# First expert of a top-1 mixture: 320 slots in the other experts' form, 128 slots stationary, a branch for 64 more

## The chip, the core and the metric

One core of one Trainium2 chip runs the whole kernel. The metric is the device time of one execution in microseconds. Engines are named as the profile names them: PE (TensorE), DVE (VectorE), ACT (ScalarE), POOL (GpSimd), SP (SyncE).

## What is computed

```python
# attention: 4 batches x 8 heads x 768 tokens x 64, float32
mask = (q_bucket == k_bucket)            # 6-bit hashes of q @ proj and k @ proj
attn = softmax(where(mask, q @ k.T / 8, -1e9));  x = attn @ v   # x: 3072 tokens x 512
# mixture, 8 experts, one expert per token
logits = x @ w_gate;  e_idx = argmax(logits)
gate_w = softmax(logits)[e_idx];  eom = sigmoid(x @ w_output_gate)
for e in range(8):
    m = e_idx == e
    h = relu(x[m] @ w1[e])               # 512 -> 1024
    out[m] = gate_w[m] * eom[m, e] * (h @ w2[e])   # 1024 -> 512
```

How many tokens an expert gets depends on the data, so the kernel sorts tokens into slots of each expert and has a general path behind it for whatever doesn't fit.

## The kernel before

Every product of the mixture is made of three matmuls (`product`, L389): both operands are split into a high and a low part, and high x high, high x low and low x high are summed. A block of 128 output columns of layer 1 over 512 inputs is thus 4 x 3 = 12 matmuls, a block of layer 2 over 1024 inputs is 8 x 3 = 24.

The experts are worked through in the order of their size. Experts 1 to 7 have one form. In layer 1 (`up`) the weights are stationary and the tokens' slots stream, as many columns as the expert's width; four steps of two blocks each write one PSUM tile `ps_s` (two buffers). ACT takes the high part (`hh`, L412), DVE the low part (`hl`, L415). In layer 2 (`down`) w2 is stationary, the slots stream again, DVE turns the result (`yt`, L452), it goes to DRAM and comes back in rows (`yo`), is scaled on ACT and scattered to the output by POOL (`send_rows`) during the next expert.

While expert r runs, its hooks prepare expert r+1 (`turned`, `next_w1`) and fetch rows for r+2. A chunk of 128 tokens is fetched by four indirect gathers `xq` (L329), issued by POOL. DVE transposes the chunk (`xt`, L342), POOL makes its high part (`xh`, L345), DVE the low part (`xlo`, L346). `pace` (L327) makes each next gather wait for the block finished last. DVE clears the PSUM tile of the next block in order behind all this work (`clear`), so the first block of expert r+1 can start only when DVE has come past expert r+1's last `xt`, `xlo` and the first half of its own `yt`. The order of each engine is the order in which the code is written; nothing reorders it.

The first expert (r = 0) is chosen while the attention still runs, as the largest after three of the four batches. It has 512 slots. The first 256 go through layer 1 during the end of the attention (`fill`, L1212: 96 matmuls of 256 columns), then through layer 2 with the slots stationary (`down_rows`: 48 matmuls of 512 columns). The other 256 are gathered, turned (`turn`, L305), go through layer 1 with the weights stationary (again 96 of 256) and layer 2 with slots stationary (`all_rows`, again 48 of 512). In this second half the hooks issue the first gathers for expert 2, after `slot_rows` has made the row numbers `idx`.

Of the kernel before, what the change touches and what calls it, by code (L numbers as in the profile page):

```python
# [33 lines left out]
WIDTHS = ((512,), (480, 448, 428), (448, 420, 404), (416, 400, 384), (384, 376, 364), (384, 364, 348),  # L34
# [6 lines left out]
CAP0 = CH * EARLY  # L41

# [25 lines left out]
def lsh_attention_then_moe(  # L68
# [73 lines left out]
    def triangle():  # L142

        trif = gp.tile([P, P], F32, name="t_tri")
# [30 lines left out]
    def load_weights(shape, src):  # L175
# [3 lines left out]
        else:  # L179

            raw = f32(gp.tile([P, NCC, CAP0], F32R, name=("xh0", "xlo0")[raws[-1] - 2])).rearrange("p a b -> p (a b)")
# [94 lines left out]
    pace = []  # L276

# [12 lines left out]
    def gather(idx, n=CH, ntok=NTOK, pool=gp, bufs=NCH):  # L290

        xg = pool.tile([CH, DM], F32, name="xg", bufs=bufs)
        nc.gpsimd.indirect_dma_start(out=xg[0:n], out_offset=None, in_=x_dram[0:ntok, :],
                                     in_offset=bass.IndirectOffsetOnAxis(ap=idx[0:n], axis=0))
        return xg, n

    def new_x0():
        return [gp.tile([P, NCC, CAP0], F32R, name=n) for n in ("xh0", "xlo0")]

    def turn(xgn, xs, c0, early=False):  # L300

        xg, n = xgn
        px = (ps_m if early else ps_t).tile([P, NCC, CH], F32, name="ps_m" if early else "ps_t")
        for cc in range(NCC):
            nc.tensor.transpose(px[:, cc, 0:n], xg[0:n].rearrange("n (p b) -> n b p", b=NCC)[:, cc], ident[0:n, 0:n])  # L305
        xh, xlo = (x[:, :, c0:c0 + n] for x in xs)
        nc.scalar.copy(xh, px[:, :, 0:n])
        nc.vector.tensor_tensor(xlo, px[:, :, 0:n], f32(xh), ALU.subtract)
# [86 lines left out]
    def up(w1s, xs, hs, fs, n, midway=None, r=None):  # L395
# [18 lines left out]
        def lows():  # L414
            nc.vector.scalar_tensor_tensor(hl, ph, 0.0, f32(hh), ALU.max, ALU.subtract)  # L415
            if r:
                clear()
            elif r == 0 and fs[-1] == NFB - 1:
                clear()
                clear()  # L420
# [9 lines left out]
    def send(r, a, n, py, sid):  # L430

        yo = mp.tile([CH, DM], F32, name="yo", bufs=4)
        nc.scalar.activation(yo[0:n].rearrange("n (a g f) -> n g a f", a=NB32, g=NCC),
                             py[0:n].rearrange("n (g a f) -> n g a f", a=NB32, g=NCC), AF.Copy,
                             scale=tacc[0:n, 1, r, a:a + 1])
        scatter(
            out=out[:, :], out_offset=bass.IndirectOffsetOnAxis(ap=sid[0:n, r, a:a + 1], axis=0),
# [18 lines left out]
    def to_dram(r, yt):  # L456

        nb = CAPS[r] // 32
        for k in range(NB32):
            nc.sync.dma_start(y_dram[0:CAPS[r], k * P:(k + 1) * P].rearrange("(t i) x -> i t x", i=32),  # L460
                              yt[32 * k:32 * k + 32, 0:nb].rearrange("i t g f -> i t (g f)"))

    def to_rows(r):

        for a, n in enumerate(chunks(r)):
# [49 lines left out]
    with ExitStack() as actx:  # L515
# [487 lines left out]
        def pick():  # L1003
# [10 lines left out]
            nc.vector.scalar_tensor_tensor(base, lead, float(CAP0), base, ALU.mult, ALU.max)  # L1014

        def lead_slots(a):

            tm = gp.tile([P, EARLY, E], F32, name="o_ls")
            nc.vector.tensor_tensor(tm, tacc_e[:, 0, :, a:a + EARLY].rearrange("p e a -> p a e"),
                                    lead[:, None, :].broadcast_to([P, EARLY, E]), ALU.mult)  # L1020
            gd = gp.tile([P, EARLY], F32, name="o_gd")
            nc.vector.tensor_reduce(gd, tm, AX.X, ALU.add)
            gid = gp.tile([P, EARLY], U32, name="gid0")
            nc.vector.tensor_scalar(gid, gd, -1.0, 0.0, ALU.add, ALU.max)
# [15 lines left out]
        def load_experts():  # L1040
# [4 lines left out]
            for i in range(1, E):  # L1045
                load_expert(idi, i)
# [45 lines left out]
        def early_gather():  # L1092
            gid = lead_slots(0)
            early["xg"] = [gather(gid[:, a:a + 1], CH, NTOK - S) for a in range(EARLY)]
# [29 lines left out]
        for a in range(EARLY):  # L1124
            plan(late + 20 + 2 * a, lambda a=a: early_turn(a))
# [86 lines left out]
        def fill(f, midway=None):  # L1212
            lows.append(up(early["w1"], early["x"], hs, [f], CAP0, midway))
# [47 lines left out]
        fill(7)  # L1261
        r["hot"]()
        r["right"]()
        rows(NP - 1, 1, False)
        low()
        r["softmax_sum"]()
        r["chosen"]()
        r["gates"]()

    mp = ctx.enter_context(tc.tile_pool(name="mp", bufs=1, reuse_waits="tile"))  # L1270
    with order_ctx:
        x0 = new_x0()
        pys = [ps_s.tile([P, 2, 512], F32, name="ps_s")[:, 0] for c in range(EARLY)]
        def first_table():
            last["table"](0, 1)
            last["entries"](0, 1)
            gid0 = lead_slots(EARLY)
            rows = [gather(gid0[:, a:a + 1]) for a in range(EARLY)]
            pick = picks()
            last["heavy"]()  # L1280
            order()
            return rows, pick

        for c in range(EARLY):
            for f in range(0, NFB, 2):
                if c == 0 and f == 2:
                    down_rows(c, CH, w2s, hs, pys[c], [f])
                    xg, pick = first_table()
                    down_rows(c, CH, w2s, hs, pys[c], [f + 1])
                else:  # L1290
                    down_rows(c, CH, w2s, hs, pys[c], [f, f + 1])
                if c == 0 and f == 6:
                    last["table"](1, 3)
                    ordered_table(0)
                    gid = sources(mp, tacc)
# [215 lines left out]
```

## Time and profile before

| | |
|---|---|
| time, median of 3 runs | 728.63 us (728.61 to 728.78) |
| the profiled execution's own time | 727.21 us |
| its span in the trace | 725.4 us |
| mean granted clock of PE | 0.997 |
| PE busy | 715.5 us (99% of the span) |
| DVE, ACT, POOL busy | 514.0, 460.0, 385.7 us |

The span is the time from the first to the last instruction of the profiled execution; 1.8 us of its own time lie around it. A share of busy time is an average over the whole span: an engine at 53% can still be the one that is waited for in a stretch of 30 us. In a timeline the busy time of a matmul overlaps the next one's; what a matmul costs is the distance between two starts.

### The profile page before, as it was taken

The page shows a single profiled execution, that of the slowest core. Times are in us where ns is not written, and L with a number is a line of the kernel's source. Part 1 is how long each engine was busy: PE and PEld are TensorE (multiplying, and loading weights), DVE is VectorE, ACT ScalarE, POOL GpSimd, SP SyncE. Part 2 cuts the span into 40 slices and gives each one's busy share as a digit, 9 for nine tenths or more (in the row PEclk, how much of TensorE's full clock was granted, in tenths as well). Part 3 has the DMA queues.
Part 4 walks back from the last instruction along what each step waited for, and adds up shares of the span by engine and source line. Part 5 has one row for each costly group of instructions (what it writes and reads, how often), then busy time and mean ns, then how long its engine had stood idle before and what let it go on. Part 6 is the DMA issues. An engine that isn't in the chain of part 4 may idle for free.

```text
span 725.4 us, 14193 instructions
## 1 busy us (share of the span) xinstructions
PE 715.5 (99%) x4671; PEld 595.9 (82%) x4671; DVE 514.0 (71%) x1148; ACT 460.0 (63%) x983; POOL 385.7 (53%) x446
## 2 busy tenths in 40 slices
PE   8999999999999999999999999999999999999996
PEld 6777767778687687776776787989999999999995
DVE  7877768878977877977899757546665647567740
ACT  8788887888877888887888762235061617153341
POOL 7655554454753554644568551455657474846212
PEclk9999999999999999999999999999999999999998
DMA  4565655555663654665465232564585867668641
GB/s 153 147 148 123 148 124 118 137 113 119 137 155 80 144 147 88 144 146 98 123 163 135 88 82 51 174 216 149 159 259 183 247 191 234 212 217 275 213 155 41
DMA packets 98020, 109.45 MB, mean 151 GB/s; under 512 B 58729, under 2 KB 70153, under 8 KB 97920
## 3 DMA queue, kind: packets, MB, share of 16 engines
q1 hardware_dynamic: 92576, 94.81, 49.4%
q0 software_dynamic: 5200, 13.31, 5.5%
q8 instruction: 60, 0.98, 0.6%
q14 instruction: 40, 0.33, 0.1%
q10 hardware_dynamic: 144, 0.02, 0.0%
HBM read 64.60 MB, written 18.32 MB: 114 GB/s over the span
## 4 chain that ended last, share of the span: by engine, by line
PE 83%; issue 6%; DVE 4%; DMA 3%; POOL 2%; SPq 1%; ACT 1%; POOLq 0%; DVEq 0%; ACTq 0%
PE ps_s L393 28%; PE ps_s L710 17%; PE ps_a L784 17%; PE ps_t L762 16%; PE ps_m L566 2%; DVE sc L714 1%; POOL out_dram L426 1%; PE ps_m L818 1%; DMA yo<-y_dram 1%; PE ps_m L393 1%; PE ps_a L393 1%; DMA yr<-xl 1%; POOL yr L612 1%; PE ps_t L305 0%; DMA xg<-x_dram,gid 0%
## 5 line engine op out<-in xcount | busy, mean ns | idle before, releaser
L746 POOL TENSOR_SCALAR sc<-sc,rsum 128x768 f32<-128x768 f32 x192 | 184.5, 975 | 182.2 <-DVE rsum L744 133.5
L714 DVE TENSOR_SCALAR_CACHE_REDUCE sc<-ps_s 128x768 f32<-128x768 f32 x192 | 181.1, 948 | 37.8 <-PE ps_s L710 32.3
L766 ACT COPY pts<-ps_t 128x384 f32<-128x384 f32 x375 | 161.3, 482 | 73.2 <-PE ps_t L762 72.6
L725 ACT ACTIVATE sc<-sc,mn 128x768 f32<-128x768 f32 (+1 forms) x223 | 187.6, 847 | 0.7 <-DVE sc L714 0.7
L762 PE MATMUL ps_t<-ident,sc 128*128 128x128 f32 x1134 | 156.7, 274 | 0.8 <-ACT pts L766 0.4
L762 PEld LDWEIGHTS ps_t<-ident,sc 128*128 128x128 f32 x1134 | 132.6, 140 | 26.4 <-POOL sc L746 10.4
L784 PE MATMUL ps_a<-pts,vt 128*64 128x384 f32 x768 | 130.9, 490 | 0.0
L412 ACT ACTIVATE hh<-ps_s 128x768 fp32r<-128x768 f32 (+6 forms) x40 | 29.3, 733 | 138.7 <-PE ps_s L393 138.7
L329 POOL DMA_INDIRECT xq<-x_dram,idx x75 | 89.5, 1193 | 52.0 <-ACT hh L412 20.0
L710 PE MATMUL ps_s<-xr,xl 128*128 128x384 f32 x384 | 114.2, 378 | 1.1 <-DVE sc L714 0.8
L784 PEld LDWEIGHTS ps_a<-pts,vt 128*64 128x64 f32 x768 | 52.3, 137 | 64.9 <-issue 56.4
L710 PE MATMUL ps_s<-yr,yl 76*128 76x384 f32 x384 | 99.3, 340 | 0.4 <-POOL yr L612 0.3
L393 PE MATMUL ps_s<-xh,w1h 128*128 128x256 f32 (+7 forms) x288 | 93.6, 325 | 0.0
L393 PE MATMUL ps_s<-xlo,w1h 128*128 128x256 f32 (+7 forms) x288 | 93.2, 324 | 0.0
L393 PE MATMUL ps_s<-xh,w1l 128*128 128x256 f32 (+7 forms) x288 | 93.1, 323 | 0.0
L415 DVE SCALAR_TENSOR_TENSOR hl<-ps_s,hh 128x768 fp32r<-128x768 f32 (+6 forms) x40 | 34.4, 859 | 62.3 <-ACT hh L412 62.3
L710 PEld LDWEIGHTS ps_s<-yr,yl 76*128 76x128 f32 x384 | 69.7, 189 | 1.0 <-POOL yr L612 0.5
L426 POOL DMA_INDIRECT out_dram<-yo,sid x27 | 28.4, 1050 | 70.2 <-ACT yo L472 55.7
L393 PE MATMUL ps_s<-hl,w2h 128*128 128x428 f32 (+5 forms) x192 | 64.8, 338 | 0.0
L393 PE MATMUL ps_s<-hh,w2h 128*128 128x428 f32 (+5 forms) x192 | 64.7, 337 | 0.0
L393 PE MATMUL ps_s<-hh,w2l 128*128 128x428 f32 (+5 forms) x192 | 64.7, 337 | 0.0
L710 PEld LDWEIGHTS ps_s<-xr,xl 128*128 128x128 f32 x384 | 58.0, 191 | 7.4 <-issue 4.9
(229 smaller groups left out, 1022.5 us busy)
## 6 DMA issues: line engine op xcount, KB each, us to landing
w_raw<-in_w_dram SPq DMA_DIRECT2D x36, 512.0 KB
qk<-in_qkT_dram SPq DMA_DIRECT2D x32, 384.0 KB
xh<-in_w_dram SPq DMA_DIRECT2D x14, 512.0 KB
xlo<-in_w_dram SPq DMA_DIRECT2D x14, 512.0 KB
vt<-in_v_dram SPq DMA_DIRECT2D x16, 384.0 KB
xr<-xl SPq DMA_DIRECT2D x30, 192.0 KB
yr<-xl SPq DMA_DIRECT2D x30, 192.0 KB
xr<-yl SPq DMA_DIRECT2D x30, 192.0 KB
```

The source lines that it names most:

```text
L329: got = nc.gpsimd.indirect_dma_start(out=xq[:, k * P:(k + 1) * P], out_offset=None, in_=x_dram.rearrange("n (a f) -> (n a) f", a=NB32), in ...
L393: nc.tensor.matmul(ps, l, r, start=first and k == 0, stop=last and k == len(pairs) - 1)
L412: pace[:] = [nc.scalar.activation(hh, ph, AF.Relu).ins]
L415: nc.vector.scalar_tensor_tensor(hl, ph, 0.0, f32(hh), ALU.max, ALU.subtract)
L426: sent = nc.gpsimd.indirect_dma_start(**k).ins
L710: nc.tensor.matmul(ss[:, n, 0:HS], l[0:k, qs], r[0:k, n * HS:(n + 1) * HS], start=first, stop=not first)
L714: nc.vector.tensor_scalar(sc, ss[:, :, 0:HS], MASKED, None, ALU.min, ALU.min, accum_out=mn)
L725: nc.scalar.activation(pr, pr, AF.Exp, bias=mn, scale=-1.0, accum_out=total)
L746: nc.gpsimd.tensor_scalar(live[s0 + k], live[s0 + k], rs[:, k:k + 1], 0.0, ALU.mult, ALU.add)
L762: nc.tensor.transpose(tr[:, c], pr[:, (3 * h + c) * P:(3 * h + c + 1) * P], ident)
L766: (nc.vector.tensor_copy if shared and h else nc.scalar.copy)(pts[:, 3 * h:3 * h + 3, t * P:(t + 1) * P], tr)
L784: nc.tensor.matmul(st["av"][j * D:(j + 1) * D], st["v"][:, j, c], blocks[hb][j][:, c], start=(c == 0), stop=(c == NT - 1))
```

## The change

The first expert's slots go from 2 x 256 to 320 "near" slots and 128 "far" slots, with a branch for 64 more. The near slots take the early place: layer 1 in `fill`, now 320 columns wide, and layer 2 in the form of the other experts (`near_down`, four output blocks of 24 matmuls; `near_back` turns them on DVE; the rows are sent during expert 1). The far slots are stationary in both layers: `far_up` (24 matmuls of 512 columns into `ps_a` and `ps_m`), `far_relu`, eight transposes of h, `far_down` (24 of 512). Three `overflow` arms hold the work of slots 448 to 511 and are skipped when these are empty. One row in two scatters is a mix of a near and a far chunk (`mixed_ids`). The row numbers `idx` are made, and the first two gathers for expert 2 issued, inside `far_down`; the other gathers of expert 2 come at expert 1's own steps. Much of the table work that follows the attention is written in another order between the matmuls.

```diff
-WIDTHS = ((512,), (480, 448, 428), (448, 420, 404), (416, 400, 384), (384, 376, 364), (384, 364, 348),
+WIDTHS = ((512, 448), (480, 448, 428), (448, 420, 404), (416, 400, 384), (384, 376, 364), (384, 364, 348),
...
+NEAR = 320
+FAR = slice(NEAR, NEAR + CH)
+UPPER = slice(CH // 2, CH)
...
-            lows.append(up(early["w1"], early["x"], hs, [f], CAP0, midway))
+            lows.append(up(early["w1"], early["x"], hs, [f], NEAR, midway))
...
         copies()
+        rows(NP - 1, 1, False)
         fill(4, lambda: r["add_pair"](1, lp))
         r["best"]()
-        low()
         r["exps"]()
         r["choose"]()
-        fill(5)
-        fill(6, r["prefix"])
         low()
+        fill(5, r["prefix"])
         r["ranks"]()
         low()
+        fill(6)
         r["cols"]()
+        r["hot"]()
+        low()
         fill(7)
-        r["hot"]()
         r["right"]()
-        rows(NP - 1, 1, False)
-        low()
-        r["softmax_sum"]()
-        r["chosen"]()
-        r["gates"]()
...
-        pys = [ps_s.tile([P, 2, 512], F32, name="ps_s")[:, 0] for c in range(EARLY)]
-        def first_table():
...
-        for c in range(EARLY):
...
+        def near_down(py, d, f0, f1):
+            ds = slice(d * P, (d + 1) * P)
+            product(py[:, d % 2, 0:NEAR], [(w[0][:, ds], w[1][:, ds]) for w in w2s[f0:f1]],
+                    [(hs[0][:, f, 0:NEAR], hs[1][:, f, 0:NEAR]) for f in range(f0, f1)], f0 == 0, f1 == NFB)
+
+        def near_back(py, dp):
+            for j in range(2):
+                nc.vector.transpose(back[:, 0:NEAR // 32, 2 * dp + j],
+                                    py[:, j, 0:NEAR].rearrange("p (t i) -> p t i", i=32))
+
+        def far_up(pu, c0):
+            for i in range(2):
+                fs = slice(i * DM, (i + 1) * DM)
+                product(pu[i], [tuple(x[:, cc, c0:c0 + CH] for x in x0) for cc in range(NCC)],
+                        [(wh[:, fs], wl[:, fs]) for wh, wl in early["w1"]])
...
+        def far_relu(ps, pu):
+            rows = [mp.tile([CH, DM], F32, name="yo", bufs=4) for i in range(2)]
+            for i in range(2):
+                pace[:] = [nc.scalar.activation(rows[i][ps], pu[i][ps], AF.Relu).ins]
+            return [rows[f // NCC][ps, f % NCC * P:(f % NCC + 1) * P] for f in range(NFB)]
...
+        def overflow():
+            return tc.If(fits[0] < 1)
...
+        near_down(py, 0, 0, 1)
+        last["table"](0, 1)
+        order()
+        last["entries"](0, 1)
+        gid0 = lead_slots(len(near) - 1, 2)
+        rest = gather(gid0[:, 0:1])
+        more = gather(gid0[:, 1:2], CH, NTOK, CH // 2)
+        pick = picks()
+        idi = experts()
+        load_expert(idi, 1)
+        raw = [w1_load(1, cc) for cc in range(2)]
+        low()
+        last["softmax_sum"]()
+        last["chosen"]()
+        last["gates"]()
+        last["heavy"]()
+        near_down(py, 0, 1, NFB)
+        near_down(py, 1, 0, 6)
+        last["table"](1, 3)
+        near_down(py, 1, 6, NFB)
+        ordered_table(0)
+        gid = sources(mp, tacc)
+        ch = chunks(1)
+        first = [gather(gid[:, 1, a:a + 1], ch[a]) for a in range(2)]
+        near_back(py, 0)
+        py = ps_s.tile([P, 2, 512], F32, name="ps_s")
+        turn(rest, x0, 0)
+        near_down(py, 2, 0, 4)
+        turn(more, x0, CH)
+        near_down(py, 2, 4, NFB)
...
+        pu = [p.tile([CH, DM], F32, name=n) for p, n in ((ps_a, "ps_a"), (ps_m, "ps_m"))]
+        far_up(pu, 0)
+        h_rest = far_relu(slice(0, CH), pu)
+        read_fit(0)
+        with overflow():
+            far_up(spill, CH // 2)
+        xn = new_x()
+        turn(first[0], xn, 0)
+        turn(first[1], xn, CH)
+        near_down(py, 3, 0, 4)
+        w1n = [w1_split(wpool, raw[0])]
...
+        for i in range(2):
+            pt = ps_t.tile([P, NCC, CH], F32, name="ps_t")
+            for k in range(NCC):
+                nc.tensor.transpose(pt[:, k], h_rest[NCC * i + k], ident)
+            pace[:] = [halves([h[:, NCC * i:NCC * (i + 1), FAR] for h in hs], pt)]
...
+        near_down(py, 3, 4, NFB)
+        near_back(py, 1)
+        clear()
+        with overflow():
+            for f in range(NFB):
+                nc.tensor.transpose(pt[:, f], h_more[f], ident[UPPER, UPPER])
+        for a in range(2, len(ch)):
+            turn(first[a], xn, a * CH)
...
+        def far_down(py, cols, fs):
+            product(py, [(hs[0][:, f, cols], hs[1][:, f, cols]) for f in fs], [w2s[f] for f in fs],
+                    fs[0] == 0, fs[-1] == NFB - 1)
...
+        far_down(py, FAR, range(0, 4))
+        idx = slot_rows(ids, pick)
+        for a in range(len(chunks(2))):
+            fetch(a, 2)
+        gather_some(2)
+        read_fit(1)
+        far_down(py, FAR, range(4, NFB))
+        send_part(py, mixed_gates, mixed_ids[:, 0:1])
+        with overflow():
+            far_down(spill, slice(0, CH), range(NFB))
+        send_part(spill, tacc[:, 1, 0, NCH - 1:NCH], mixed_ids[:, 1:2])
+        over, nri = rounds()
+        w1s, xs = w1n, xn
+
+        for r in range(1, E):
+            n = CAPS[r]
...
-                if r == 0 and fp == 0:
-                    for a in range(2, len(nxt)):
-                        xgs[1, a] = gather(gid[:, 1, a:a + 1])[0], nxt[a]
-                elif r:
-                    gather_some(2)
+                gather_some(2)
...
-            if r == 0:
-                idx = slot_rows(ids, pick)
-                for a in range(len(chunks(2))):
-                    fetch(a, 2)
-                over, nri = rounds()
...
-                if r:
-                    gather_some(STEPS[i])
-                elif i < NCH:
-                    gather_some(1 if i else 2)
-                elif i % 2 == 0:
-                    gather_some(1)
+                gather_some(STEPS[i])
```

The first place is the end of the first expert and the beginning of expert 1 in POOL's order. L329 (L338 after) are the gathers `xq`, L293 whole-row gathers for expert 1, L426 (L432) scatters to the output; a branch of L384 (L393) marks the end of a matmul group of expert 1. Before:

```order
L293 DMA xg<-x_dram,gid 128x512 x2
L329 DMA xq<-x_dram,idx 128x128 x5
L426 DMA out_dram<-yo,sid 3072x512
L329 DMA xq<-x_dram,idx 128x128 x2
L384 UNCONDITIONAL_BRANCH x2
L426 DMA out_dram<-yo,sid 3072x512
L329 DMA xq<-x_dram,idx 128x128 x2
L384 UNCONDITIONAL_BRANCH
L329 DMA xq<-x_dram,idx 128x128 x2
```

and after the change:

```order
L338 DMA xq<-x_dram,idx 128x128 x2
L1426 UNCONDITIONAL_BRANCH
L393 UNCONDITIONAL_BRANCH x2
L432 DMA out_dram<-yo,mixed_ids 3072x512 x2
L338 DMA xq<-x_dram,idx 128x128 x2
L393 UNCONDITIONAL_BRANCH
L338 DMA xq<-x_dram,idx 128x128 x2
L393 UNCONDITIONAL_BRANCH
L432 DMA out_dram<-yo,sid 3072x512 x2
L338 DMA xq<-x_dram,idx 128x128 x2
L354 TENSOR_SCALAR xh<-xt 128x4x128
L432 DMA out_dram<-yo,sid 3072x512
```

Seven gathers for expert 2 stood ahead of expert 1's first step and now two do; five scatters of the first expert now stand among expert 1's gathers, where one stood.

The second place is the rows that follow in POOL's order (two gathers lie between). Before:

```order
L345 TENSOR_SCALAR xh<-xt 128x4x128
L329 DMA xq<-x_dram,idx 128x128 x2
L384 UNCONDITIONAL_BRANCH
L345 TENSOR_SCALAR xh<-xt 128x4x128
L329 DMA xq<-x_dram,idx 128x128
L345 TENSOR_SCALAR xh<-xt 128x4x128
L329 DMA xq<-x_dram,idx 128x128 x2
L345 TENSOR_SCALAR xh<-xt 128x4x64
```

and after, from the scatter on:

```order
L393 UNCONDITIONAL_BRANCH
L338 DMA xq<-x_dram,idx 128x128 x2
L354 TENSOR_SCALAR xh<-xt 128x4x128
L338 DMA xq<-x_dram,idx 128x128 x2
L354 TENSOR_SCALAR xh<-xt 128x4x128
L338 DMA xq<-x_dram,idx 128x128
L393 UNCONDITIONAL_BRANCH
L338 DMA xq<-x_dram,idx 128x128
L393 UNCONDITIONAL_BRANCH
L354 TENSOR_SCALAR xh<-xt 128x4x64
```

The four `xh` are the chunks 0 to 3 of expert 2 (4, 4, 4 and 2 gathers). The last of these 14 gathers stood ahead of the second `xh`; now two of them stand between the third and the fourth.

The third place is the first skipped arm on PE (L1366), with what each row waits for. Before, the same place held 96 matmuls of 256 columns without a branch. After:

```order
L377 TENSOR_LOAD o_armi [waits DVE_49]
L377 ISA x2
L1366 COMPARE_AND_BRANCH
L402 MATMUL ps_s<-w1h,xh_6359 128x512 [waits DVE_49,PE_49,Activation_49]
...
L1366 UNCONDITIONAL_BRANCH
L1366 UNCONDITIONAL_BRANCH [waits PE_49]
L310 MATMUL ps_t<-ident,xg 128x128 [waits DMASW5_49,PE_49]
L310 MATMUL ps_t<-ident,xg 128x128 x3
```

The first branch row closes the arm that is skipped, the second is the arm that runs instead; it waits for PE's own earlier matmuls to have ended. The arms at L1385 and L1426 end in the same way.

## Rows read from the trace of the kernel before

**Rows 1.** The page: busy time (us, share, instructions); chain that ended last, by engine.

```profile
PE 715.5 (99%) x4671; PEld 595.9 (82%) x4671; DVE 514.0 (71%) x1148; ACT 460.0 (63%) x983; POOL 385.7 (53%) x446
...
PE 83%; issue 6%; DVE 4%; DMA 3%; POOL 2%; SPq 1%; ACT 1%; POOLq 0%; DVEq 0%; ACTq 0%
```

**Rows 2.** Timeline of TensorE: start, busy us, instruction; spacing of matmuls by width.

```profile
460.63 0.28 PE L393 MATMUL ps_s<-xh,w1h 128*128 128x256 f32 x1
460.75 0.28 PE L393 MATMUL ps_s<-xlo,w1h 128*128 128x256 f32 x1
...
479.86 0.40 PE L393 MATMUL ps_a<-w2h,hh 128*128 128x512 f32 x1
480.09 0.39 PE L393 MATMUL ps_a<-w2l,hh 128*128 128x512 f32 x1
...
485.42 0.35 PE L393 MATMUL ps_s<-xh,w1h 128*128 128x428 f32 x1
...
522.44 0.35 PE L393 MATMUL ps_s<-xh,w1h 128*128 128x420 f32 x1
...
657.65 0.32 PE L393 MATMUL ps_s<-xh,w1h 128*128 128x340 f32 x1
657.81 0.32 PE L393 MATMUL ps_s<-xlo,w1h 128*128 128x340 f32 x1
```

**Rows 3.** Timeline of TensorE at the two transposes of the first expert's later slots.

```profile
455.82 0.40 PE L393 MATMUL ps_s<-w2h,hl 128*128 128x512 f32 x1
456.27 0.75 PE L305 MATMUL ps_t<-ident,xg 128*128 128x128 f32 x4
...
458.25 0.64 PE L305 MATMUL ps_t<-ident,xg 128*128 128x128 f32 x4
458.64 0.48 PE L393 MATMUL ps_s<-w2h,hh 128*128 128x512 f32 x1
```

**Rows 4.** Timeline of GpSimd around and in expert 1.

```profile
476.03 0.94 POOL L329 DMA_INDIRECT xq<-x_dram,idx  x1 [11.13 <-DVE over L1073]
...
491.55 0.97 POOL L329 DMA_INDIRECT xq<-x_dram,idx  x1 [2.60 <-ACT hh L412]
492.83 1.81 POOL L329 DMA_INDIRECT xq<-x_dram,idx  x1 [0.30 <-issue]
...
503.18 0.62 POOL L345 TENSOR_SCALAR xh<-xt 128x512 fp32r<-128x512 f32 x1 [0.20 <-DVE xt L342]
```

**Rows 5.** Timeline of GpSimd in expert 2, whose first matmul is at 522.44.

```profile
538.98 1.02 POOL L426 DMA_INDIRECT out_dram<-yo,sid  x1 [2.93 <-ACT yo L472]
```

**Rows 6.** DMA issues: gathers of 484 to 526 us, at 491.55, at 523.70; median us to landing.

```profile
xq<-x_dram,idx POOLq DMA_INDIRECT x18, 3.7
...
xq<-x_dram,idx POOLq DMA_INDIRECT x1, 2.5
...
xq<-x_dram,idx POOLq DMA_INDIRECT x1, 5.2
```

**Rows 7.** Timeline of VectorE at the end of expert 1.

```profile
509.54 1.08 DVE L342 STREAM_TRANSPOSE xt<-xq 128x512 f32<-128x512 f32 x1
...
512.85 0.64 DVE L342 STREAM_TRANSPOSE xt<-xq 128x256 f32<-128x256 f32 x1
513.40 1.19 DVE L194 TENSOR_TENSOR w1l<-w_raw,w1h 128x1024 fp32r<-128x1024 f32 x1
...
516.23 1.24 DVE L452 STREAM_TRANSPOSE yt<-ps_s 128x480 f32<-128x480 f32 x2
517.56 0.13 DVE L364 MEMSET ps_s<- 128x88 f32 x1
...
518.72 1.22 DVE L194 TENSOR_TENSOR w1l<-xlo,w1h 128x1024 fp32r<-128x1024 f32 x1
```

**Rows 8.** Windows after the last matmul: engine busy us, then PEclk, DMA share, GB/s.

```profile
719.00:720.00 1.00, 0.38 (x4) 0.16 (x2) 0.00 (x0) 0.47 (x1) 0.00 (x0) 1.00 0.15 42
...
721.00:722.00 1.00, 0.00 (x0) 0.00 (x0) 0.00 (x0) 0.00 (x0) 0.11 (x1) 0.77 0.29 80
```

More of the change, by code (lines that the diff above doesn't have):

```diff
@@ L276, in lsh_attention_then_moe @@
     pace = []
+    near = [min(CH, NEAR - c) for c in range(0, NEAR, CH)]
     def sources(pool, tacc):
@@ L1092, in early_gather @@
         def early_gather():
-            gid = lead_slots(0)
-            early["xg"] = [gather(gid[:, a:a + 1], CH, NTOK - S) for a in range(EARLY)]
+            gid = lead_slots(0, len(near))
+            early["xg"] = [gather(gid[:, a:a + 1], n, NTOK - S) for a, n in enumerate(near)]
         def early_turn(a):
@@ L1123, in lsh_attention_then_moe @@
                     plan_ahead(late + 27 + 2 * n, lambda n=n: early_lo(NCC - 1, n))
-        for a in range(EARLY):
-            plan(late + 20 + 2 * a, lambda a=a: early_turn(a))
+        for a in range(len(near)):
+            plan(late + 18 + 2 * a, lambda a=a: early_turn(a))
         order_ctx.enter_context(tc.manual_schedule(engines=MANUAL))
@@ L1272, in lsh_attention_then_moe @@
         x0 = new_x0()
-        pys = [ps_s.tile([P, 2, 512], F32, name="ps_s")[:, 0] for c in range(EARLY)]
-        def first_table():
[L1275 to L1282, printed above, removed]
-        for c in range(EARLY):
[L1285 to L1295, printed above, removed]
-                    first = [gather(gid[:, 1, a:a + 1])[0] for a in range(2)]
-                    sid = targets(mp, tacc)
-                    last["entries"](1, 3)
-                    ordered_table(1)
-                    ids = mp.tile([P, E * NCH], F32R, name="ids")
-                    nc.vector.tensor_scalar(ids, tacc[:, 0].rearrange("p e a -> p (e a)"), -1.0, 0.0, ALU.add, ALU.max)
-                    load_experts()
-                    narrower()
-                if c and f == 0:
-                    send(0, 0, CH, pys[0], sid)
-                if c and f in (2, 4):
-                    turn(xg[f // 4], x0, f // 4 * CH)
@@ new lines, in lsh_attention_then_moe @@
+        ch = chunks(1)
+        first = [gather(gid[:, 1, a:a + 1], ch[a]) for a in range(2)]
+        near_back(py, 0)
+        py = ps_s.tile([P, 2, 512], F32, name="ps_s")
+        turn(rest, x0, 0)
+        near_down(py, 2, 0, 4)
+        turn(more, x0, CH)
+        near_down(py, 2, 4, NFB)
+        first += [gather(gid[:, 1, a:a + 1], ch[a]) for a in range(2, len(ch))]
+        last["entries"](1, 3)
+        ordered_table(1)
+        sid = targets(mp, tacc)
+        narrower()
+        for i in range(2, E):
+            load_expert(idi, i)
@@ new lines, in lsh_attention_then_moe @@
+        raw = [w1_load(1, cc) for cc in range(2, NCC)]
+        near_down(py, 3, 4, NFB)
[6 more added lines that the diff above has]
+            turn(first[a], xn, a * CH)
+        w1n.append(w1_split(wpool, raw[0]))
+        clear()
+        w1n.append(w1_split(wpool, raw[1], "l"))
+        halves([h[:, :, UPPER] for h in hs], pt)
@@ L1410, in lsh_attention_then_moe @@
                 back = None
[L1411 to L1415 removed]
+                for a in range(len(ch)):
+                    if a == len(ch) - 1:
                         last_rows(r, a, ch[a], w2s, hs, sid)
                     else:
[L1418 removed]
+                        all_rows(r, a, a, ch[a], w2s, hs, sid, between)
             split()
```

137 lines of the change are left out of this document (74 added, 63 removed).

## Prediction

> **What bounds the kernel now.** I read the page first: PE is busy 715.5 of 725.4 us and carries 83% of the chain that ended last [rows 1]. So what is taken off PE is gained, as long as PE then waits for nothing new. Next the timeline of PE, for what a matmul costs by the distance of two starts [rows 2]. 256 columns: 460.75 - 460.63 = 0.12 us (0.118 over longer stretches, which I use). 512 columns: 480.09 - 479.86 = 0.23 (0.2315). 428 columns: 192 matmuls from 485.42 to 522.44, 37.02 us, 0.193 each. 340 columns: 657.81 - 657.65 = 0.16. Cost follows the columns, with little fixed part. Then the timelines of POOL and VectorE in expert 1 and at its end [rows 4, 7], because the order of POOL there is what the change disturbs: DVE clears the first PSUM tile of expert 2 at 517.56 to 517.69, and PE wants it at 522.44 [rows 2]. That margin, 4.75 us, is all that separates the preparation of expert 2 from the critical path.
>
> **What goes and comes on PE.** Removed are 192 matmuls of 256 columns (96 early, 96 late) and 96 of 512: 192 x 0.118 + 96 x 0.2315 = 22.66 + 22.22 = 44.88 us. Added: layer 1 of the near slots, 96 of 320 columns, and layer 2, 4 x 24 of 320; no row has 320, so I take it between 256 and 340 in proportion, 0.147. The far slots add 24 + 24 of 512. Sum: 192 x 0.147 + 48 x 0.2315 = 28.22 + 11.11 = 39.33. Difference -5.55 us.
>
> Eight transposes of h are new. Four transposes take 458.64 - 458.25 = 0.39 us from start to the next start [rows 3], so eight take 0.8. Three early gathers are turned in place of two: +0.4. The old wait for the late gather goes: the matmul at 455.82 should free PE at 456.05, and the transposes start at 456.27 [rows 3], so -0.2; the new order asks for these rows one output block later, after 48 near matmuls.
>
> Three skipped arms are new. Each makes PE wait until its own earlier matmuls have ended, so the next one can't overlap. No row shows such a wait. From below it is nothing. From above, the busy time of a 512-column matmul is 0.40 where its spacing is 0.23 [rows 2], so 0.17 of a matmul is outstanding when the next starts; with a branch besides I bound it at 0.5 each. Nearest to the row is 0.2 to 0.3; I take 0.3, in all +0.9 (0 to 1.5). A skip can't gain, since it holds no work that was there before.
>
> The rows of h pass relu on ACT, transposes, and two halves before `far_down` wants them; 24 near matmuls and the transposes of expert 1's rows (some 24 x 0.147 + 16 x 0.1 = 5 us) lie between, so I cost that chain at nothing (0 to 1). The tables written in another order lie beside 48 near matmuls in the same way: 0 (-0.3 to 0.5). Sum for the first expert: -5.55 + 0.8 + 0.4 - 0.2 + 0.9 = **-3.65 us** (-4.9 to -1.6).
>
> **What is late next: the gathers of expert 2.** Call U the start of expert 1's first matmul; its 192 matmuls last 37.0 us [rows 2], so PE wants the next tile at U+37.0. Before, seven gathers were issued by about then, the first at 476.03, 9.4 us ahead of U [rows 4]. After, two are. One gather holds POOL 0.94 to 0.97 us, up to 1.81 [rows 4], with 0.30 of idle before the next: 1.25 at best. The pairs at steps 1 and 2 are paced by PE as before (491.55 is U+6.1). At step 3 two scatters of the near rows stand ahead. Expert 2 has that pattern today: 538.98 is 16.5 us after its start at 522.44 [rows 2, 5]. From here POOL is counted in its written order:
> scatters U+16.5 and 17.9, each 1.02 and 0.30, done 19.2; gathers 7 and 8 until 21.4; `xh` 0 of 0.62 [rows 4] until 22.2; the third scatter until 23.5; gathers 9 and 10 until 26.0; `xh` 1 until 26.7; gathers 11 and 12, the latter issued at 28.2; landing 3.7 later, the median [rows 6]: 31.9. DVE's `xt` of chunk 2, 1.08 [rows 7]: 33.0. `xh` 2: 33.7. Only then gathers 13 and 14, the latter issued at 35.1 and landed at 38.8. Then DVE: `xt` 3, w1l and `xlo` 3, some 2.1 us (0.64, 1.19, and a short last one, overlapping) and from 516.23 to 517.69 the first `yt` pair and the clearing, 1.46 [rows 7]: tile ready at U+42.3. PE stands from 37.0: **+5.3 us**. The two w1l behind the clearing end 2.25 us later (519.94 in [rows 7]), while PE reaches the last of them after 11 matmuls of 0.19: +0.2.
> The bounds: both landings at 2.5 take 2.4 off, both at 5.2 add 3.0 [rows 6]; two of the eight gathers at the 1.81 of the long one add 1.7. So 2.9 to 10, and 5.3 by the median.
>
> The Trainium skill (SBUF — State Buffer, section "SBUF: two separate sides") says that DVE and GpSimd share a port pair that one instruction locks whole. The trace's 0.97 and 1.81 of two neighbouring gathers [rows 4] agree with something of that kind; by it, gathers beside DVE's two-input work would all go to the long value, and the stall toward its upper bound.
>
> At the boundary of experts 2 and 3 POOL starts late: the five gathers for expert 3 that follow the first `yt` now end some 6 us into expert 2, where its first paced pair is due at U2+6. They catch up within a step; I take +0.2 (0 to 2).
>
> **The clock.** PE's clock shows what such a stall costs besides. The last matmul ends at 719.38, and in the window from 721 the granted clock averages 0.77 [rows 8]: one level down, from 2.4 to 1.2 GHz, at about 721.5, so 2.1 us after the work ended. A wait of 5.3 us is longer, so PE would come back at half speed. No row shows a rise after a wait. If it takes as long as the fall, 2.1 us of half speed lose 1.0; bounds 0 and, at twice that, 2.1. I take **+1.0**.
>
> The Trainium skill (TensorE: Matmul & The Clock Gate, section "HAM oscillation — how this bites in real kernels") says the same: a wait for data throttles the engine, and the work after it starts cold. The fall in the trace agrees; the cost after a wait no run here shows.
>
> **Sum.** -3.65 + 5.3 + 0.2 + 0.2 + 1.0 = +3.05 us on the profiled execution's own 727.21 (725.4 of span and 1.8 around it): 730.3. The median of the runs is 728.63, 1.4 above that execution; the same +3.05 gives **731.7 us** by the median.
>
> **Rivals.**
> A, the stall stays small (the other side). The place is the end of gather 14. With landings near 2.5, as the gather at 491.55 had [rows 6], and 1.25 per issue, the tile is ready at U+39.9, 2.9 late. Two microseconds less in POOL's chain (scatters ready sooner than in expert 2, because the near rows come back while nothing else loads) and it is below 1 us late, with no clock loss: -3.65 + 0.9 = -2.7, so 725.9. For it: the margin of 4.75 us that DVE has today, and that POOL has idle stretches of 1.5 to 2.6 us ahead of its paced gathers [rows 4]. Against: two landings stand one behind the other in the written order, and neither can be hidden. It decides from a stall below about 2.2 us, where the kernel gets faster than 728.63.
> B, gain and stall cancel: stall 2.5 to 4 with little clock loss, +0.4 at the middle: 729.0.
> C, the backlog grows: long gathers, late landings, clock low for longer, and expert 3 late also: -3.65 + 8 + 2 + 1.5 = +7.9, 736.5. For it: 1.81 in [rows 4] and 5.2 in [rows 6]. Against: after expert 2 nothing is new on POOL.
> D, the arms run. The branch is taken only above 448 tokens; worked out from the inputs the first expert has 435 tokens. If they ran, 48 more matmuls of 512 would add 11 us: 740.
>
> **How the numbers follow.** Forecast 0.48, A 0.24, B 0.14, C 0.13, D 0.01. About 0.2%, 1.46 us, is what a measurement of this kernel can tell from no change. All of A but a little lies below 727.2; B lies within 0.2%, with a small part of A and of the forecast; the rest above 730.1. That makes faster 0.23, the same 0.17, slower 0.60. The likeliest case has its own range of 729.5 to 735 (stall 3 to 8). The range that leaves out 2 in 10 reaches down into A and a little into C: 726.0 to 735.5.
>
> **What would show it.** First matmul of expert 1 earlier by about 3.7 us than 485.42: the first expert's sum. In expert 1, POOL without idle from the third pair of gathers on, gather 14 issued after the third `xh`. A wait of PE of about 5 us before expert 2's first matmul, released by DVE's clearing, and a window after it with a granted clock under 1. Each arm a gap of 0.2 to 0.4 on PE. Wrong would be: no PE wait at that boundary, a wait at the first expert's transposes of h, or a wait at the boundary of experts 2 and 3 as long as the first.

## The result and the profile after

The changed kernel takes 733.36 us (median of 6, 732.53 to 734.34) against 728.70 for the kernel before on the same chip: ratio 1.0066, 95% interval 1.0053 to 1.0079. It is slower, by 4.7 us where +3.0 was forecast. Its profiled execution took 734.34 us (span 732.6), at the top of that range, and the one of before 727.21, so the two traces lie 7.1 us apart.

I read the waits of PE over the whole execution first: total us, times, longest.

```profile
PE ps_s L402 <- DVE ps_s L373: 5.8, 2, 5.0
...
PE ps_s L402 <- DVE hl L424: 0.6, 1, 0.6
PE ps_s L402 <- PEq L1426: 0.4, 1, 0.4
PE ps_s L402 <- DVE yt L460: 0.4, 1, 0.4
...
PE ps_t L310 <- PEq L1385: 0.4, 1, 0.4
PE ps_t L310 <- PEq L1366: 0.3, 1, 0.3
```

One wait of 5.0 us for the clearing of a tile, three of 0.3 to 0.4 at the three skipped arms, and little else (0.4 at expert 3, 0.6 in expert 5, and the second wait of the first line, 0.75 in expert 6). The timeline of PE has the places; [rows 2] are the same matmuls of before.

```profile
469.11 1.22 PE L310 MATMUL ps_t<-ident,xg 128*128 128x128 f32 x8 [0.30 <-PEq L1366]
...
475.09 1.18 PE L310 MATMUL ps_t<-ident,xg 128*128 128x128 f32 x8 [0.38 <-PEq L1385]
...
482.74 0.45 PE L402 MATMUL ps_s<-xh,w1h 128*128 128x428 f32 x1 [0.44 <-PEq L1426]
...
524.94 0.69 PE L402 MATMUL ps_s<-xh,w1h 128*128 128x420 f32 x1 [5.02 <-DVE ps_s L373]
525.43 0.55 PE L402 MATMUL ps_s<-xlo,w1h 128*128 128x420 f32 x1
525.78 0.55 PE L402 MATMUL ps_s<-xh,w1l 128*128 128x420 f32 x1
...
564.46 0.42 PE L402 MATMUL ps_s<-xh,w1h 128*128 128x400 f32 x1 [0.40 <-DVE yt L460]
```

Expert 1 starts 2.7 us earlier than before (482.74 against 485.42), expert 2 2.5 us later (524.94 against 522.44), after 5.02 us of waiting. Then the matmuls of expert 2 stand 0.35 us apart in place of 0.19. The windows say why: us, busy time (instructions) of PE, PEld, DVE, ACT, POOL, then PEclk, DMA share, GB/s; [rows 8] are two such rows.

```profile
522.00:524.00 2.00, 0.00 (x0) 0.00 (x0) 1.70 (x4) 0.00 (x0) 0.95 (x1) 0.82 0.20 31
524.00:525.00 1.00, 0.06 (x1) 0.09 (x1) 0.91 (x4) 0.00 (x0) 0.00 (x0) 0.50 0.76 217
525.00:530.00 5.00, 5.00 (x15) 4.75 (x16) 3.33 (x5) 0.00 (x0) 3.92 (x4) 0.50 0.71 235
530.00:531.00 1.00, 1.00 (x6) 0.98 (x5) 0.00 (x0) 0.00 (x0) 0.69 (x2) 0.94 0.97 305
531.00:532.00 1.00, 1.00 (x7) 0.98 (x7) 0.00 (x0) 0.00 (x0) 0.78 (x1) 1.00 1.01 273
```

The granted clock goes down during the wait, to 1.2 GHz, and is back at 2.4 GHz only when PE has worked for some 5 us (0.94 in the window from 530). Layer 1 of expert 2 takes 20.71 us (524.94 to 545.65) against 18.41 before.

Who made the tile late is read on POOL and DVE together. POOL, gathers 11 to 14 of expert 2 and the `xh` between them (of before, [rows 4]):

```profile
509.26 1.41 POOL L338 DMA_INDIRECT xq<-x_dram,idx  x1 [0.16 <-issue]
510.97 0.96 POOL L338 DMA_INDIRECT xq<-x_dram,idx  x1 [0.30 <-issue]
514.76 1.50 POOL L354 TENSOR_SCALAR xh<-xt 128x512 fp32r<-128x512 f32 x1 [2.84 <-DVE xt L351]
516.43 1.41 POOL L338 DMA_INDIRECT xq<-x_dram,idx  x1 [0.16 <-issue]
518.14 0.96 POOL L338 DMA_INDIRECT xq<-x_dram,idx  x1 [0.30 <-issue]
521.67 1.29 POOL L354 TENSOR_SCALAR xh<-xt 128x256 fp32r<-128x256 f32 x1 [2.56 <-DVE xt L351]
```

and DVE, which waits for the landings and clears the tile last (of before, [rows 7]):

```profile
513.60 1.08 DVE L351 STREAM_TRANSPOSE xt<-xq 128x512 f32<-128x512 f32 x1 [3.78 <-DMA xq<-x_dram,idx]
514.60 1.19 DVE L198 TENSOR_TENSOR w1l<-w_raw,w1h 128x1024 fp32r<-128x1024 f32 x1
...
520.96 0.62 DVE L351 STREAM_TRANSPOSE xt<-xq 128x256 f32<-128x256 f32 x1 [3.96 <-DMA xq<-x_dram,idx]
...
523.33 1.24 DVE L460 STREAM_TRANSPOSE yt<-ps_s 128x480 f32<-128x480 f32 x2
524.66 0.13 DVE L373 MEMSET ps_s<- 128x88 f32 x1
```

Two landings (the time from a gather's issue until its rows are in SBUF) stand one behind the other: gather 12 (510.97) lands for DVE's `xt` at 513.60, the third `xh` follows, only then are gathers 13 and 14 issued, and DVE waits for these until 520.96.

### The profile page after: what moved, and what is told of

Its sections match the earlier page's. It is cut to its first block, busy times and chain, and to the rows that moved or that the text cites. A ratio compares the mean times of both kernels' runs of the same rounds, so it can differ in the third digit from the quotient of the medians.

```text
span 732.6 us, 14169 instructions
## 1 busy us (share of the span) xinstructions
PE 715.5 (98%) x4635; PEld 595.1 (81%) x4635; DVE 519.7 (71%) x1160; ACT 462.9 (63%) x988; POOL 394.4 (54%) x451
## 5 line engine op out<-in xcount | busy, mean ns | idle before, releaser
L421 ACT ACTIVATE hh<-ps_s 128x768 fp32r<-128x768 f32 (+5 forms) x36 | 27.4, 761 | 139.1 <-issue 68.7
L338 POOL DMA_INDIRECT xq<-x_dram,idx x75 | 89.3, 1191 | 30.9 <-issue 19.6
L402 PE MATMUL ps_s<-xh,w1h 128*128 128x320 f32 (+7 forms) x256 | 86.7, 339 | 6.6 <-DVE ps_s L373 5.8
L402 PE MATMUL ps_s<-xlo,w1h 128*128 128x320 f32 (+7 forms) x256 | 85.9, 335 | 0.0
L402 PE MATMUL ps_s<-xh,w1l 128*128 128x320 f32 (+7 forms) x256 | 85.6, 334 | 0.0
L402 PE MATMUL ps_s<-hh,w2h 128*128 128x320 f32 (+6 forms) x224 | 75.5, 337 | 0.1
L402 PE MATMUL ps_s<-hl,w2h 128*128 128x320 f32 (+6 forms) x224 | 74.6, 333 | 0.6 <-DVE hl L424 0.6
L402 PE MATMUL ps_s<-hh,w2l 128*128 128x320 f32 (+6 forms) x224 | 74.5, 332 | 0.0
L424 DVE SCALAR_TENSOR_TENSOR hl<-ps_s,hh 128x768 fp32r<-128x768 f32 (+5 forms) x36 | 32.1, 891 | 50.7 <-ACT hh L421 37.4
L432 POOL DMA_INDIRECT out_dram<-yo,sid x26 | 27.6, 1063 | 69.0 <-ACT yo L481 56.4
```

The source lines that it names most:

```text
L338: got = nc.gpsimd.indirect_dma_start(out=xq[:, k * P:(k + 1) * P], out_offset=None, in_=x_dram.rearrange("n (a f) -> (n a) f", a=NB32), in ...
L402: nc.tensor.matmul(ps, l, r, start=first and k == 0, stop=last and k == len(pairs) - 1)
L421: pace[:] = [nc.scalar.activation(hh, ph, AF.Relu).ins]
L432: sent = nc.gpsimd.indirect_dma_start(**k).ins
```

## The experiments

Each ratio is to the kernel before on the same chip, with its 95% interval; the changed kernel stands at 1.0066.

**Two pairs of gathers moved in POOL's order.** Gathers 9 to 12 in one go, so that 11 and 12 stand ahead of the second `xh`, and 13 and 14 ahead of the third:

```diff
-                gather_some(2)
+                gather_some(4 if r == 1 and fp == 3 else 2)
...
-                gather_some(STEPS[i])
+                gather_some(2 if r == 1 and i == 0 else STEPS[i])
```

> The changed kernel with the same two gathers ahead of expert 1, but gathers 9 to 12 issued together and 13 and 14 ahead of the third xh instead of behind it. Theory (two landings of some 3.7 us stand one behind the other in POOL's order): one landing goes from the chain, the stall falls from 5.0 to about 1 us, the clock does not fall, time 733.4 - 4 - 2.5 = about 727 (726 to 728.5). Rival (POOL is simply out of time: the sum of its issues sets the end, not the landings): the stall stays at 4 us or more and the time at 732 or more.

Measured: 726.24 us, 0.9973 (0.9963 to 0.9982). With no other edit the slower kernel is faster than before. POOL and PE of this kernel:

```profile
511.56 1.41 POOL L338 DMA_INDIRECT xq<-x_dram,idx  x1 [0.16 <-issue]
513.27 0.96 POOL L338 DMA_INDIRECT xq<-x_dram,idx  x1 [0.30 <-issue]
514.26 0.80 POOL L354 TENSOR_SCALAR xh<-xt 128x512 fp32r<-128x512 f32 x1
515.22 1.41 POOL L338 DMA_INDIRECT xq<-x_dram,idx  x1 [0.16 <-issue]
516.93 1.59 POOL L338 DMA_INDIRECT xq<-x_dram,idx  x1 [0.30 <-issue]
518.55 0.41 POOL L354 TENSOR_SCALAR xh<-xt 128x256 fp32r<-128x256 f32 x1
```

```profile
520.96 0.43 PE L402 MATMUL ps_s<-xh,w1h 128*128 128x420 f32 x1 [1.20 <-DVE ps_s L373]
```

Gathers 13 and 14 are now issued at 511.56 and 513.27, ahead of the third `xh` at 514.26; POOL no longer idles for a landing, PE waits 1.20 us, and the granted clock stays 1.00 after it. The rest of the wait can be seen too: two gathers for expert 3 (515.22, 516.93) stand ahead of the fourth `xh`.

**The last `xh` first.** The same, with no gathers at the two hooks ahead of the fourth `xh`:

```diff
-                gather_some(2 if r == 1 and i == 0 else STEPS[i])
+                gather_some(((2, 0, 0, 2) + STEPS[4:] if r == 1 else STEPS)[i])
```

> The kernel with gathers 9 to 14 ahead (the version before) and, beside it, the fourth xh written ahead of the two gathers for expert 3 that stood before it. In the version before PE still waited 1.2 us at the start of expert 2, and the trace has the fourth xh behind two gathers of 1.4 and 1.6 us on POOL. Theory (POOL's written order alone makes that rest): the fourth xh ends 1.5 us earlier, the wait goes, time 726.2 - 1.2 = about 725.0. Rival (DVE, with w1l behind the last xt, sets the end): the wait stays over 0.8 us, time 726.2.

Measured: 725.14 us, 0.9962 (0.9948 to 0.9976); the wait is 0.22 us. In the trace it is as the theory had it; the two intervals overlap, so the microsecond is shown by the wait and not by the times.

**PE kept busy.** Twenty matmuls that nobody reads between experts 1 and 2:

```diff
+            if r == 1:
+                idle = ps_m.tile([P, 512], F32, name="ps_m")
+                for k in range(20):
+                    nc.tensor.matmul(idle, w2s[0][0][:, 0:P], w2s[k % NFB][0][:, 0:512], start=True, stop=True)
```

> The changed kernel with 20 matmuls of 512 columns, 4.6 us of work whose result nobody uses, on PE between expert 1's last matmul and expert 2's first. They fill the stall and delay nothing if it is 5.0 us. Theory (the slow matmuls of the 5 us after the stall come from the clock, which falls because PE stands idle): the granted clock stays 1.00 there, the stall shrinks to about 0.4 us with the end where it was, time 733.4 - 2.5 = about 730.9. Rival (the matmuls after the stall are slow for another reason, such as the transfers that run beside them): no change, 733.4, or more.

Measured: 731.27 us, 1.0040 (1.0027 to 1.0053). PE, and the window after:

```profile
519.96 4.72 PE L1503 MATMUL ps_m<-w2h 128*128 128x512 f32 x20
525.24 0.43 PE L402 MATMUL ps_s<-xh,w1h 128*128 128x420 f32 x1 [0.56 <-DVE ps_s L373]
```

```profile
525.00:530.00 5.00, 4.76 (x25) 4.55 (x26) 3.63 (x6) 0.00 (x0) 3.63 (x4) 1.00 0.67 229
```

The tile comes as late as before (525.24), but the same window has 25 matmuls at a granted clock of 1.00 in place of 15 at 0.50, and layer 1 of expert 2 is back at 18.42 us. Extra work made the kernel 1.9 us faster by the ratios (0.0026 of 728.7); layer 1 gives 2.3 in the trace. The transfers beside them are much the same (229 GB/s in place of 235), so the slow matmuls are the clock's doing, and the clock's fall is the wait's.

**Which part of the change makes the wait.** The kernel before, with two gathers ahead of expert 1 in place of seven and nothing else:

```diff
-                elif i < NCH:
-                    gather_some(1 if i else 2)
-                elif i % 2 == 0:
-                    gather_some(1)
+                elif i < 1:
+                    gather_some(2)
```

> The kernel before the change, with two gathers for expert 2 ahead of expert 1 in place of seven; nothing else is changed. This is the one part of the change that puts the gathers late, without its scatters. Theory (late gathers and the scatters among them add up on POOL): a stall at the start of expert 2 of 1 to 2.5 us, the clock mostly kept, time 728.7 + 1.8 = about 730.5. Rival (the place of the gathers alone makes the whole stall): a stall near 5 us and the clock down after it, 735 or more. Second rival (the scatters alone): no stall, 728.7.

Measured: 734.62 us, 1.0087 (1.0072 to 1.0102). My theory missed: the first rival held, with a wait near 5 us and a granted clock of 0.52 in the 5 us after it. PE and POOL of this kernel:

```profile
527.85 0.69 PE L393 MATMUL ps_s<-xh,w1h 128*128 128x420 f32 x1 [4.53 <-DVE ps_s L364]
```

```profile
511.49 0.96 POOL L329 DMA_INDIRECT xq<-x_dram,idx  x1 [0.30 <-issue]
516.57 1.50 POOL L345 TENSOR_SCALAR xh<-xt 128x512 fp32r<-128x512 f32 x1 [4.12 <-DVE xt L342]
...
519.94 0.96 POOL L329 DMA_INDIRECT xq<-x_dram,idx  x1 [0.30 <-issue]
524.58 1.28 POOL L345 TENSOR_SCALAR xh<-xt 128x256 fp32r<-128x256 f32 x1 [3.68 <-DVE xt L342]
```

Without the scatters POOL issues gather 12 at 25.4 us into expert 1 (486.13 its start) in place of 28.2, but then stands idle 4.12 and 3.68 us for landings, in place of 2.84 and 2.56. The landings of gathers 12 and 14 took 3.9 us each in place of 2.6 and 2.8, which took back most of what the scatters had cost; why they took longer I can't say. It is the written order behind too few early gathers that makes the wait: 4.5 us of it come without any other part of the change.

**Scatters behind the gathers of their step**, in the changed kernel:

```diff
+                        if r == 1:
+                            gather_some(2)
                         for _ in range(2):
                             if whole:
                                 send_rows(*whole.pop(0), sid)
                 split()
-                gather_some(2)
+                gather_some(0 if r == 1 and fp >= 2 else 2)
```

> The changed kernel with the three scatters of the near rows written behind the pair of gathers of their step in expert 1 instead of ahead of it; the fifth pair then stands ahead of the third scatter too. Theory (what stands ahead of the gathers on POOL counts by its own time): gathers 9 and 10 come some 3 us earlier, of which the third scatter takes 1.3 back before the second xh, stall 5.0 - 2 = about 3 us, the clock down for a shorter time, time 729.5 to 732. Rival (gathers are paced by PE's blocks there and the scatters cost nothing): no change, 733.4.

Measured: 731.27 us, 1.0047 (1.0034 to 1.0060), but the wait is 4.95 us in the trace: the wait that I expected to shrink did not. Gathers 9 and 10 did go out 2.3 and 1.7 us earlier (503.86 and 505.76 in place of 506.18 and 507.49). But gather 12 goes out at 510.56, only 0.4 us earlier than in the changed kernel, since the moved scatters stand ahead of it all the same, and gather 14 then takes 3.3 us to land in place of 2.8. The time lies in the range of the theory even so; by the wait that is luck. The intervals of the two ratios overlap, and what the 1.4 us between them hang on stays open.

**Without the arms.** The changed kernel without the three `overflow` blocks:

```diff
-        read_fit(0)
-        with overflow():
-            far_up(spill, CH // 2)
...
-        with overflow():
-            for f in range(NFB):
-                nc.tensor.transpose(pt[:, f], h_more[f], ident[UPPER, UPPER])
...
-        with overflow():
-            far_down(spill, slice(0, CH), range(NFB))
```

> The changed kernel without its three overflow arms and without the read of the first expert's count on PE (slots 448 to 511 are then not computed; they are empty on these inputs). Theory (each skipped arm makes PE wait for its own matmuls to end, 0.30, 0.38 and 0.44 us in the trace, and nothing else): the gaps go, expert 1 starts 1.1 us earlier, the stall is as long as before, time 733.4 - 1.1 = about 732.3. Rival (the arms also hold back other engines, or cover work that is then waited for): the gain is under 0.4 us, or over 2 us.

Measured: 731.05 us, 1.0038 (1.0025 to 1.0051), 2.0 us less by the ratios, with intervals too wide to tell it from 1.1. The trace can tell. The matmuls behind the three arms, without them:

```profile
468.64 1.12 PE L310 MATMUL ps_t<-ident,xg 128*128 128x128 f32 x8
...
474.00 1.09 PE L310 MATMUL ps_t<-ident,xg 128*128 128x128 f32 x8
...
480.97 0.35 PE L402 MATMUL ps_s<-xh,w1h 128*128 128x428 f32 x1
```

The far slots' first matmul starts alike in both traces (463.04 here, 463.05 with the arms). With the arms the three lines come at 469.11, 475.09 and 482.74, so 0.47, 1.09 and 1.77 us later. An arm thus costs 0.47, 0.62 and 0.68 us, more than its gap of 0.30, 0.38 and 0.44. The rest, some 0.2 us each, is the lost overlap of two matmuls: the last 512 columns ahead of the first arm are busy for 0.40 us where the next start would come after 0.23. So the theory that the gaps are the whole cost missed. The wait at expert 2 is as long as ever, 5.38 us.

**The best version** joins the two: last `xh` first, a cap of 448 slots for the first expert and no arms, so that more tokens than that would take the general path.

```diff
-WIDTHS = ((512, 448), (480, 448, 428), (448, 420, 404), (416, 400, 384), (384, 376, 364), (384, 364, 348),
+WIDTHS = ((448,), (480, 448, 428), (448, 420, 404), (416, 400, 384), (384, 376, 364), (384, 364, 348),
...
-        with overflow():
-            far_down(spill, slice(0, CH), range(NFB))
-        send_part(spill, tacc[:, 1, 0, NCH - 1:NCH], mixed_ids[:, 1:2])
```

> The same, with the first expert's cap set to 448 slots, so that the three arms, their zeroed tiles, copies and the second mixed scatter go (more tokens would take the general path at the end). Theory (arms cost their three gaps, 0.30, 0.30 to 0.38 and 0.44 us on PE, one scatter fewer gives POOL 1.3 us): 1.1 us less than the version before, about 723.9. Rival (a new wait takes the place of the gaps): no more than 0.4 us less.

Measured: 723.52 us, 0.9944 (0.9931 to 0.9956), 4.1 us under the kernel before. PE has one wait left in the whole mixture, 0.20 us. This is what the change is worth without the arms, when nothing waits.

**Seven gathers ahead again.** Five more behind `far_down`:

```diff
         far_down(py, FAR, range(4, NFB))
+        gather_some(5)
```

> The changed kernel with five more gathers for expert 2 issued behind far_down, so that seven stand ahead of expert 1's first step as before the change. Theory (the stall of 5.0 us at the start of expert 2 comes from the 14 gathers being issued too late, and the half-speed clock of 2.5 us from the stall): PE waits under 0.5 us there, the granted clock stays 1.00 in 515 to 540 us, time 733.4 - 5.0 - 2.5 = about 725.9 (725 to 727). Rival (the five scatters of the first expert among expert 1's gathers are what POOL is late by, not the place of the gathers): a stall of 2 to 4 us stays, time 729 to 733.

Measured: 729.83 us, 1.0018 (1.0008 to 1.0027). The wait at expert 2 is gone, as the theory says, but its time is missed by 4 us: a new wait of 3.40 us stands inside expert 1, with a granted clock of 0.50 from 503 to 505 us behind it. There the second relu, on ACT, came at 498.37 though its matmuls had ended at 492.7 (48 of 0.193 us from 483.42). Three more versions went after that. The first keeps the seven gathers. Twelve one-element copies on ACT, written ahead of the near slots' layer 2, move its program:

```diff
+        for k in range(12):
+            nc.scalar.copy(pad, pad)
         near_down(py, 0, 0, 1)
...
+        gather_some(5)
```

> The kernel with seven gathers ahead of expert 1 again, with twelve one-element copies more on ACT, written ahead of the near slots' layer 2, where ACT has time. In that kernel's trace the second relu of expert 1 came at 498.37 us, 5.6 us after its matmuls had ended, and PE waited 3.4 us behind it; the second relu of expert 6 was late too. Theory A (that wait hangs on where ACT's instructions lie in its program, not on the gathers): with ACT's program moved by twelve the wait of expert 1 is gone or elsewhere, time about 726 to 727.5. Theory B (the seven gathers delay something that the relu needs): the wait of about 3.4 us stays at the same relu, time 729.8.

Measured: 730.18 us, 1.0015 (1.0002 to 1.0027); the relu came at 498.61. Theory B held. Then the two mixed scatters first, the five gathers behind them:

```diff
+        gather_some(5)
         over, nri = rounds()
         w1s, xs = w1n, xn
```

> Seven gathers for expert 2 ahead of expert 1's first paced pair again, but with the two mixed scatters left where the change has them, behind the second gather, and the other five gathers behind the scatters. With the scatters behind all seven, their buffers came free late, and the read-back of the near rows on SP and the w1 loads behind it went out at 495 to 497 us in place of 492 to 493. Theory (that late chain, not the number of gathers, made PE wait 3.4 us inside expert 1): no wait inside expert 1 nor at the start of expert 2, time 733.4 - 5.0 - 2.5 = about 726 (725 to 727.5). Rival (seven gathers at that place make the wait in any order): a wait of 2 us or more inside expert 1, time 728.5 to 730.

Measured: 730.10 us, 1.0019 (1.0009 to 1.0029); the wait is 2.99 us, the rival held: SP's loads went out at 492.42 and the relu was late all the same, at 497.52. What the three kernels have in common is that POOL issues without a break (its row), and the relu comes 1.65 to 1.76 us after the end of that row. So three gathers in place of the five:

```diff
-        gather_some(5)
+        gather_some(3)
```

> As the version with the mixed scatters first, but with three gathers behind them in place of five: five gathers for expert 2 stand ahead of expert 1's first paced pair. With seven, POOL issued nine gathers and two scatters without a break until 495.9 us, and the second relu of expert 1 came 1.65 us behind that, in three kernels alike (1.65 to 1.76), though its matmuls had ended at 492. Theory A (the relu is held until POOL's unbroken row has ended): the row ends 2.5 us earlier, the relu comes at about 495, PE waits under 0.6 us inside expert 1, and no wait is left at the start of expert 2: 733.4 - 7.5 + 0.5 = about 726.4. Theory B (the two have nothing to do with each other): the relu is at about 492.3 or still near 497.5. With it at 497.5: 730; at 492.3: 725.9.

Measured: 726.19 us, 0.9960 (0.9944 to 0.9975). The row's last gather and the relu, first with five, then with three:

```profile
494.92 0.95 POOL L338 DMA_INDIRECT xq<-x_dram,idx  x1 [0.30 <-issue]
```

```profile
497.52 0.97 ACT L421 ACTIVATE hh<-ps_s 128x960 fp32r<-128x960 f32 x1 [6.89 <-PE ps_s L402]
```

```profile
492.41 0.95 POOL L338 DMA_INDIRECT xq<-x_dram,idx  x1 [0.30 <-issue]
```

```profile
495.05 0.97 ACT L421 ACTIVATE hh<-ps_s 128x960 fp32r<-128x960 f32 x1 [4.42 <-remote]
```

The row ends 2.5 us earlier, and so does the relu, at 495.05 where about 495 was expected. Theory A's figures came in, but for a wait of PE of 0.69 us in place of under 0.6. Its cause is not shown. The relu comes 2.60 to 2.73 us after the start of the row's last gather in the four kernels, so it may as well hang on that gather's landing. And a row doesn't hold every relu: with seven gathers ahead, the first relu of expert 1 starts at 488.39, inside the row of 482.48 to 496.70. What passes from POOL to ACT the trace doesn't say: one line names PE, whose matmuls had ended, the other an unnamed "remote".

## Why the prediction was right

**The first expert: -2.7 us, forecast -3.65.** The price of 320 columns is right: 0.147 between starts. The term that was mis-sized is the arms: 1.77 us by the version without them, where the forecast had 0.9 and at most 1.5. The prediction took the gap alone (1.1 of the 1.77), though its own 0.17 of a matmul still outstanding comes on top of it. The third early turn is in the 0.7 us by which the first near matmul comes later (421.66 against 420.93, forecast 0.4). The other terms are right: from the first near matmul to expert 1 the version without arms takes 59.3 us, the kernel before 64.5, so 5.2 less where they add up to -4.95. No wait came at the transposes of h or in the table work, as forecast.

**The wait: 5.0 us, forecast 5.3.** The count along POOL's written order held place by place: gather 12 goes out 28.2 us into expert 1 (forecast 28.2), gather 14 at 35.4 (35.1), the tile is ready at 42.1 (42.3). Inside, two sizes were off and cancelled, which is luck. Landings took 2.6 and 2.8 us in place of 3.7, so 2.0 less. POOL's third `xh` took 1.50 in place of 0.62 and the gather behind it 1.41, so that from the end of `xt` to the issue of gather 14 it was 3.5 us in place of 2.1. DVE's work after the last landing took 0.3 more than counted. The kernel before had the same `xh` and gather at the same place:

```profile
510.71 1.50 POOL L345 TENSOR_SCALAR xh<-xt 128x512 fp32r<-128x512 f32 x1 [0.24 <-DVE xt L342]
512.37 1.41 POOL L329 DMA_INDIRECT xq<-x_dram,idx  x1 [0.16 <-issue]
```

The prediction took its 0.62 from the first `xh` instead [rows 4]. In the changed kernel the third `xh` begins 0.16 us behind DVE's w1l, which runs 1.19. The Trainium skill (SBUF — State Buffer, section "SBUF: two separate sides") says that of two such instructions the loser blocks for the whole of the other. The trace agrees nearly: 1.19 - 0.16 + 0.62 = 1.65, against the 1.50. All gathers at the long value, as the prediction drew from that section, didn't come: of gathers 7 to 14 two took 1.41 us and six 0.95 to 1.00.

My reading that the three scatters matter was weaker than the sum made it look: without them the wait is 4.53. What decides is that gathers 13 and 14 stand behind an `xh` that waits for gather 12; moved ahead of it, with 11 and 12 one `xh` earlier too, they leave a wait of 1.20.

**The clock: +2.3 us, forecast 1.0.** The mechanism was right, as the filled wait shows; the size was not. The step that failed is the assumption that the clock rises as fast as it fell; PE worked some 5 us at 1.2 GHz before it was back, and layer 1 of expert 2 took 2.3 us longer. That is beyond the bound of 2.1. The Trainium skill (TensorE: Matmul & The Clock Gate, section "HAM oscillation — how this bites in real kernels") has the work after a data wait start cold; these runs now show it, and what a filled wait gives back.

**Experts 2 to 7.** The wait at expert 3 is 0.40 (forecast 0.2). Not forecast are 0.57 and 0.75 us in experts 5 and 6 of this trace. The second comes behind a late second relu (674.47, 0.75 us after a row of POOL's had ended), as in several of the other versions' traces (waits of 0.3 to 1.0 us), but in neither the best version nor the kernel before. In the best version that relu starts at 661.69, 1.5 us before such a row ends. I couldn't settle what decides it.

The sum at the start of expert 3 is -2.7 + 5.0 + 2.3 + 0.4 + 0.3 (the first matmuls behind the waits) = +5.3, and the trace has 564.46 - 559.10 = +5.4; the two late waits and what belongs to them bring the traces to 7.2 apart. By the medians it is +4.7, and 733.36 lies in the likeliest case's own range. So the total is right in its direction and its two main terms, while the wait's exact size owes something to luck, and arms and clock cost more than forecast. Rival A had the landings right (near 2.5), and fell on what the prediction put against it, two landings in the written order that nothing hides, and on the slow `xh` and gather between them. Rival D's 740 adds the arms' 11 us to the kernel before; on the forecast of 731.7 it would have been some 743.

## What to carry to other kernels

Before a change takes PE work out, count what the other engines issue in the stretch that gets shorter, in their written order: here 5.5 us of matmuls went (by the forecast's sum) and 5.0 us of waiting came, since five gathers had lost their place. An order in which a transfer is issued behind an instruction that waits for an earlier transfer pays both landings; moving two pairs of gathers ahead by one `xh` took most of the wait back and won 2 us on the kernel before. And count a wait of PE of this length one and a half times: here 5.0 us of waiting brought 2.3 us of slow matmuls after it.

## What the runs showed of the hardware

After 5.0 us without work PE ran some 5 us at 1.2 GHz; a wait of 1.2 us (gathers ahead) left the clock at 2.4. Waits of 3.40 and 2.99 us (seven gathers ahead; five behind the scatters) left it at 2.4 until PE had started again, and then it fell to 1.2 for some 3 us (0.50 from 503 to 505 us in the one trace, from 501 to 504 in the other). Twenty matmuls that nobody needs, 4.7 us of them in place of the wait of 5.0, kept it at 2.4. A skipped branch that ends in a wait for PE's own matmuls leaves a gap of 0.30 to 0.55 us on PE in these traces, and cost 0.47 to 0.68 us against the version without it. And the second relu of expert 1, whose matmuls had ended, came 1.65 to 1.76 us after POOL's unbroken row of indirect DMAs in four kernels; other relus start inside such rows, and why stays open.
